# A planned attention kernel: a pace for background steps, either added copy on GpSimd, quartered projections, a new table of limits

## The chip, the cores and the metric

The kernel runs on one core of one Trainium2 chip. The metric is device time in microseconds (us) for one execution. The core has five engines with queues of their own, which wait for each other only by semaphores: TensorE (PE in the profile, with its weight loads as PEld), VectorE (DVE), ScalarE (ACT), GpSimd (POOL), and SyncE (SP), which issues the transfers here. TensorE writes into PSUM, eight banks of 128 x 512 fp32; the other data live in SBUF.

## The reference, cut to what matters

Four layers follow each other, each adding to x (2048 tokens, 512 features, 32 heads of 16 features): A, B, A, B.

```python
x = A_x
x = x + _A_ref(_layernorm(x), A_wq, A_wk, A_wv, A_wo, A_beta)
x = x + _B_ref(_layernorm(x), B_wqkv, B_wo)
x = x + _A_ref(_layernorm(x), A_wq, A_wk, A_wv, A_wo, A_beta)
x = x + _B_ref(_layernorm(x), B_wqkv, B_wo)
```

B is plain attention of all 2048 tokens with all. A cuts the tokens into four segments of 512 with causal attention inside each, and mixes in a memory of the segments before, weighed by a gate g:

```python
logits = jnp.einsum('bhqd,bhkd->bhqk', qs, ks) * scale + mask
a_dot = jnp.einsum('bhqk,bhkd->bhqd', _softmax(logits), vs)
num = jnp.einsum('bhld,bhde->bhle', phi(qs), M)
den = jnp.einsum('bhld,bhd->bhl', phi(qs), z)[..., None] + 1e-06
o = g * (num / den) + (1.0 - g) * a_dot
M = M + jnp.einsum('bhld,bhle->bhde', phi(ks), vs)
z = z + jnp.einsum('bhld->bhd', phi(ks))
```

Both end in a projection with wo. The exponentials of the softmax are most of the work outside TensorE: two B layers have 4 query segments x 4 chunks of heads x 2 x 64 banks of scores each, 4096 in all; two A layers have 16 pairs of groups of 20 banks each, 640 in all.

## The kernel before, in words

The program is one long order of instructions that a planner in Python writes out while it builds. `Sched.estimate` (line 128) keeps an estimated clock for every engine (`sc.t`), and what comes next is decided by comparing these clocks with limits. What the planner estimates never reaches the chip; only the order that it chose does.

*Units.* `attention` (2048) goes through units. A unit takes up to three banks of scores (`take_banks`, 1698): TensorE computes them into one of two sets of three PSUM banks, ScalarE makes the exponential of the unit in one instruction (line 1790), and two units later TensorE multiplies by the values (`pv`, 1810) into a bank of sums. One PSUM bank more (`misc_bank`) serves the projections and everything else in the background.

*VectorE's banks.* Some banks don't go to ScalarE. If `ring_open` (1208) allows, one of a unit's three banks is VectorE's; if `dx_open` (1200) allows, the unit has two banks for ScalarE and two for VectorE, the extra one in `misc_bank`. So 1540 units hold 4736 banks. For such a bank VectorE computes an approximate exponential by integer arithmetic: `dx_first` (1286, recorded at line 1294) reads the scores out of PSUM into a 16-bit number whose bits are a bf16 near the exponential; two added copies, shifted by the constants of `EXP_STEPS` (36 and 84), follow, and TensorE multiplies all three by the values and sums them, in place of one product. The copies are made by `task_dx` (1332) for up to two banks at a time (line 1350) and by `dx_four` (1368) for four (line 1382). The second copy may go to GpSimd: `pool_copy` (1357, recorded at line 1364) treats two 16-bit numbers as one 32-bit integer and adds a constant held in the tile `shift`, provided GpSimd's estimated clock isn't over `POOL_C` ns ahead of VectorE's. It waits for the first copy too (`first`). The three parts are held in the tiles dxt, and, once they are free, in KA, QA, VA and the weights wA and wB.

*Background.* Layer norm, projections, memory, output projections and loads are generators (`task_A` 904, `task_mem` 956, `task_B` 1018, `task_out` 1105, `task_load` 1082) that yield before each step what the step needs, how many column blocks of TensorE and how many ns of VectorE it takes. After each unit `background` (1512) calls `bg_one` (1461), which runs the first step that may go by credits and limits. A projection (`proj_fm` 862, `proj_tm` 874) is four accumulating products of 512 columns, in two pieces: `PART` before a yield of "cont", the rest after it. While a "cont" is open, no four-bank unit starts and the two banks `misc_bank` and `sums_bank` aren't swapped. `wide` is set in `dx_widen` (1263) when the first A layer is done; before it the pieces are always two and two.

*Limits.* `PLAN` (366) has a row for every 20 units ("stretch", `set_limits` 2043); a name that a row doesn't set has its default. Those that the prediction speaks of: POOL_C as above; POOL_XN and POOL_QM give the normalizing step and the query masks to GpSimd; PART and OPART cut projections; PAIRS, NEAR, LOW, R_NEAR say how many banks must be ready ahead before VectorE gets some; DX_LATE, R_LATE, DVE_LATE how far VectorE may lag behind.

The gate for an extra VectorE bank in a unit, as an example of how the limits work:

```python
if not self.RING or self.near < self.rush() and self.pending() or self.low or self.near < self.R_NEAR or self.step - max(self.ring_step, self.dx_step) < self.RGAP or len(self.dx_pairs) - self.dx_waits() > self.R_PAIRS or self.late("act") < self.ACT1:
    return False
```

Of the kernel before, what the change touches and what calls it, by code (L numbers as in the profile page):

```python
# [362 lines left out]
class Builder:  # L363
# [3 lines left out]
        0: dict(TAKEN_A=1, FILL_DVE=200, MASK_PE=800, PE_LOW=7, GAP=3, BG_BANK=400, QMIN=3),  # L367
        1: dict(TAKEN_A=1, FILL_DVE=200, MASK_PE=800, PE_LOW=7, GAP=1, BG_BANK=400, QMIN=3, LOW=20),
        2: dict(EVAC_ACT=800, NEAR=5, SLACK=350, R_NEAR=10, BACK=6, CARRY_W=400, NEARW=40, OPART=3, PAIRS=60, DIV_LATE=2500, BUSY_WAIT=0, TAKEN=0.3, DVE_LATE=800, BUSY_BACK=800, R_PAIRS=2),
        3: dict(EVAC_ACT=800, NEAR=5, SLACK=350, R_NEAR=10, BACK=6, CARRY_W=400, NEARW=40, OPART=3, PAIRS=60, DIV_LATE=2500, BUSY_WAIT=0, TAKEN=0.3, DVE_LATE=800, BUSY_BACK=800, R_PAIRS=2, MARGIN=600),  # L370
        4: dict(MARGIN=500, DX_BANK=900, NEAR=8, SLACK=550, EARLY=300, FILL=0.42, CR_B=1200, PART=3, NEARW=20, PAIRS=60, BUSY_WAIT=0, DX_FIN=3000, POOL_QM=1, POOL_XN=1, EVAC_ACT=800, R_NEAR=10, BACK=6, CARRY_W=400, OPART=3, TAKEN=0.3, DVE_LATE=800, BUSY_BACK=800),
        5: dict(MARGIN=500, DX_BANK=900, NEAR=8, SLACK=550, EARLY=300, FILL=0.42, CR_B=1200, PART=3, NEARW=20, PAIRS=60, BUSY_WAIT=0, DX_FIN=3000, POOL_QM=1, POOL_XN=1, EVAC_ACT=800, R_NEAR=10, BACK=6, CARRY_W=400, OPART=3, TAKEN=0.3, DVE_LATE=800, BUSY_BACK=800, LOW=20),
        6: dict(ACT1=400, NEAR=8, TAKEN_A=1, SLACK=550, PV_SKIP=900, FILL_DVE=200, BACK=8, CR_W=1900, NEARW=20, OPART=2, TAKEN=0.4, LOW=14, DVE_LATE=800, QWAIT=8, HOLD_AT=40, PHI_LATE=0, REST=12),
        7: dict(MARGIN=350, R_LATE=1500, DX_LATE=900, TAKEN_A=1, EARLY=300, CARRY_W=1500, PART=3, OPART=3, MASK_PE=800, GAP=3, QUAD=0, QWAIT=3, HOLD_SEGS=2, POOL_XN=1),
        8: dict(R_LATE=1200, NEARW=40, PAIRS=24, MASK_PE=800, LEVEL=3, TAKEN=0.5, LOW=30, MARGIN=350, TAKEN_A=1, EARLY=300, OPART=3, QUAD=0, FILL=0.47, DX_BANK=900, CR_A=1200),
        9: dict(R_LATE=1200, NEARW=40, PAIRS=24, MASK_PE=800, LEVEL=3, TAKEN=0.5, LOW=30, MARGIN=350, TAKEN_A=1, EARLY=300, OPART=3, FILL=0.47, DX_BANK=900, CR_A=1200, HOLD_SEGS=2),
        10: dict(ACT1=400, DX_BANK=700, NEAR=18, BACK=3, CR_W=1900, CR_B=1800, R_PAIRS=2, PAIRS=24, DIV_LATE=800, DVE_LATE=800),
        11: dict(R_LATE=1500, DX_LATE=900, REST=12, NEAR=8, TAKEN_A=1, R_NEAR=50, PV_SKIP=500, FILL_DVE=400, BUSY_ROOM=900, CR_W=1300, DX_LAG=1, LOW=20, HOLD_SEGS=2, BACK=6),
        12: dict(R_LATE=1500, DX_LATE=900, REST=12, NEAR=8, TAKEN_A=1, R_NEAR=50, PV_SKIP=500, FILL_DVE=400, BUSY_ROOM=900, CR_W=1300, DX_LAG=1, LOW=20, HOLD_SEGS=2, BACK=6, DVE_LATE=800, EARLY=500),
        13: dict(ACT1=600, NEAR=10, PV_SKIP=200, DX_LAG=3, MASK_PE=800, LEVEL=3, DIV_LATE=2500, BG_BANK=100, QUAD=0),  # L380
        14: dict(ACT1=400, REST=16, NEAR=3, SLACK=350, R_NEAR=10, EARLY=0, FILL_DVE=200, BUSY_ROOM=300, CR_B=1800, R_PAIRS=2, PAIRS=999, TAKEN=0.3, QWAIT=8, QMIN=3, HOLD_AT=12, LN1_AT=6, CR_A=1200, MARGIN=500, DVE_LATE=800),
        15: dict(MARGIN=400, NEAR=12, PV_SKIP=100, FILL_DVE=100, BUSY_ROOM=300, FILL=0.55, CR_W=1500, CARRY_W=400, R_PAIRS=2, OPART=3, GAP=3, DVE_LATE=800, QMIN=1, HOLD_AT=40, POOL_QM=1, PAIRS=24),
        16: dict(NEAR=12, BACK=2, CR_W=1300, NEARW=40, DX_LAG=1, DIV_LATE=2500, BUSY_WAIT=0, TAKEN=0.3, DVE_LATE=800, QWAIT=3, QMIN=4, HOLD_MAX=0, PHI_LATE=300, MARGIN=400, FILL_DVE=100, R_PAIRS=2, GAP=3, HOLD_AT=40),
        17: dict(ACT1=200, DX_LATE=500, NEAR=10, PV_SKIP=200, EARLY=500, FILL=0.53, CR_B=1800, CARRY_W=1500, OPART=2, DX_LAG=1, MASK_PE=800, LEVEL=3, DIV_LATE=800, DVE_LATE=800, BG_BANK=100, QUAD=0, LN1_AT=6, POOL_XN=1),
        18: dict(ACT1=400, DX_BANK=700, NEAR=18, BACK=3, CR_W=1900, CR_B=1800, R_PAIRS=2, PAIRS=24, DIV_LATE=800, DVE_LATE=800, EARLY=500, FILL=0.53, CARRY_W=1500, MASK_PE=800, BG_BANK=100, POOL_XN=1),
        19: dict(ACT1=400, DX_BANK=700, NEAR=18, BACK=3, CR_W=1900, CR_B=1800, R_PAIRS=2, PAIRS=24, DIV_LATE=800, DVE_LATE=800, POOL_C=1500),
        20: dict(DX_BANK=900, SLACK=700, PV_SKIP=100, FILL_DVE=200, BUSY_ROOM=300, BACK=10, FILL=0.47, CR_W=1500, PART=3, R_PAIRS=2, TAKEN=0.3, DVE_LATE=800, LN1_AT=3, BUSY_BACK=800),
        21: dict(DX_BANK=900, SLACK=700, PV_SKIP=100, FILL_DVE=200, BUSY_ROOM=300, BACK=10, FILL=0.47, CR_W=1500, PART=3, R_PAIRS=2, TAKEN=0.5, DVE_LATE=800, LN1_AT=3, BUSY_BACK=800, POOL_XN=1),
        22: dict(DX_BANK=900, SLACK=700, PV_SKIP=100, FILL_DVE=200, BUSY_ROOM=300, BACK=6, FILL=0.47, CR_W=1500, PART=3, R_PAIRS=2, TAKEN=0.5, DVE_LATE=800, LN1_AT=3, BUSY_BACK=800, POOL_XN=1, EARLY=300, DIV_LATE=2500),
# [78 lines left out]
    PART = 2  # L468
# [393 lines left out]
    def proj_fm(self, w, bw, off, slot, c, dst, bdst, need=()):  # L862
# [242 lines left out]
    def task_out(self, L, s):  # L1105
        isA = L % 2 == 0
        wo, bwo = (self.woA, self.b_woA) if isA else (self.woB, self.b_woB)
        for ti in range(4):
# [23 lines left out]
            for n, (a, c, ba) in enumerate(srcs):  # L1132
                if half and n == self.OPART:
                    yield ["cont"], NCH - n, 700
# [1065 lines left out]
```

## Time and profile before

| | us |
|---|---|
| median of 3 runs (lowest, highest) | 1719.71 (1719.31, 1720.13) |
| the profiled execution, its own time | 1720.15 |
| its span, first to last instruction | 1718.4 |
| mean granted TensorE clock | 1.00 of full speed |

The page counts an engine as busy while an instruction of it runs; overlapping instructions count once in a group's busy time, and a mean is over single durations, so count times mean can exceed busy. "Idle before, releaser" is the time in which the engine waited just before that group, and what ended it. Stretches of 43 us show where each engine works (columns: TensorE, its weight loads, VectorE, ScalarE, GpSimd, each with its instructions, then the granted clock, the share of the transfer engines and GB/s):

```profile
129.00:172.00 43.00, 40.58 (x534) 16.81 (x528) 34.09 (x72) 43.00 (x37) 10.38 (x13) 1.00 0.10 20
946.00:989.00 43.00, 41.54 (x606) 19.01 (x606) 29.31 (x56) 42.91 (x37) 16.73 (x26) 1.00 0.36 90
1419.00:1462.00 43.00, 39.86 (x411) 10.09 (x407) 41.80 (x64) 42.77 (x48) 25.53 (x26) 1.00 0.03 7
```

VectorE is less busy in the first 300 us, where layer norms and projections must come before there is much attention to do, and again around the middle, where the second pair of layers begins; from about 1250 us on the last layer's attention fills the engines.

### The profile page before, as it was taken

To read this page: it belongs to the slowest core of one execution; us is meant where nothing else is said; L and a number is where in the kernel's file an instruction comes from. 1 tells how busy PE (TensorE), PEld (TensorE's weight loads), DVE (VectorE), ACT (ScalarE), POOL (GpSimd) and SP (SyncE) were. 2 spreads that over 40 slices of the span, in tenths; PEclk is the share of its full clock that TensorE was granted. 3 is DMA by queue.
4 is the path that set the end of the run, shared out by engine and by line. 5 is a ranking of instruction groups with operands and counts; after the bars stand their busy time and mean duration, and the time that the engine had idled before them with its cause. 6 is when DMAs were issued, how large, how long until landed. Compare 5 with 4: busy or idle time off the path is not lost.

```text
span 1718.4 us, 45396 instructions
## 1 busy us (share of the span) xinstructions
PE 1610.9 (94%) x19708; PEld 578.9 (34%) x19775; DVE 1460.6 (85%) x2623; ACT 1681.9 (98%) x1586; POOL 736.1 (43%) x825
## 2 busy tenths in 40 slices
PE   8999899999999999999999999999999999999998
PEld 5543335232222233423342442442222222222236
DVE  6757677989999989789889689797699999998995
ACT  8999999999999999999999999999999999999997
POOL 3222412345557545422413333443266566565651
PEclk9999999999999999999999999999999999999999
DMA  6211202001111000211211311011011100100000
GB/s 179 39 20 20 45 14 33 11 11 26 47 29 26 11 14 20 63 47 26 53 33 45 90 21 50 17 24 35 20 23 23 32 14 7 26 11 11 23 14 18
DMA packets 148425, 54.47 MB, mean 32 GB/s; under 512 B 128768, under 2 KB 147712, under 8 KB 148224
## 3 DMA queue, kind: packets, MB, share of 16 engines
q1 hardware_dynamic: 148224, 51.56, 13.7%
q8 instruction: 155, 2.54, 0.6%
q14 instruction: 46, 0.38, 0.1%
HBM read 18.88 MB, written 2.10 MB: 12 GB/s over the span
## 4 chain that ended last, share of the span: by engine, by line
ACT 67%; PE 17%; DVE 13%; issue 1%; DMA 1%; POOL 1%; SPq 0%; another core or an unknown queue 0%; ACTq 0%; DVEq 0%
ACT pT L1790 65%; PE ps L622 17%; DVE dxt L1294 2%; DVE KA L1294 1%; DVE wA L1294 1%; ACT amem L890 1%; DVE wB L1294 1%; DVE QA L1382 1%; DVE lnst L794 1%; POOL xn L823 0%; SPq L691 0%; DVE wA L1382 0%; DVE dxt L1382 0%; DVE dxt L1350 0%; DMA xT<-xn 0%
## 5 line engine op out<-in xcount | busy, mean ns | idle before, releaser
L1790 ACT ACTIVATE pT<-ps 128x1024 bf16<-128x1024 f32 (+1 forms) x1540 | 1650.2, 1257 | 22.3 <-PE ps L622 19.8
L622 PE MATMUL ps<-qm,KB 32*128 32x512 bf16 x4096 | 565.2, 384 | 72.6 <-ACT pT L1790 47.2
L622 PE MATMUL ps<-pT,VB 128*17 128x512 bf16 x2892 | 494.4, 384 | 1.6 <-DVE dxt L1294 0.5
L622 PEld LDWEIGHTS ps<-qm,KB 32*128 32x128 bf16 x4096 | 144.9, 91 | 595.1 <-ACT pT L1790 476.8
L1294 DVE TENSOR_SCALAR KA<-ps 128x512 uint16<-128x512 f32 (+1 forms) x396 | 291.9, 757 | 14.8 <-PE ps L622 11.8
L1364 POOL TENSOR_TENSOR VA<-KA,shift 128x512 int32<-128x512 int32 (+1 forms) x193 | 200.1, 1047 | 231.0 <-DVE QA L1350 144.6
L1364 POOL TENSOR_TENSOR dxt<-dxt,shift 128x512 int32<-128x512 int32 (+1 forms) x143 | 149.3, 1052 | 282.9 <-DVE dxt L1350 197.5
L1294 DVE TENSOR_SCALAR dxt<-ps 128x512 uint16<-128x512 f32 (+1 forms) x307 | 218.9, 729 | 19.2 <-PE ps L622 17.6
L622 PEld LDWEIGHTS ps<-pT,VB 128*17 128x17 bf16 x2892 | 115.5, 87 | 283.9 <-issue 271.9
L622 PE MATMUL ps<-dxt,VB 128*17 128x512 bf16 x945 | 206.5, 381 | 0.0
L1804 POOL TENSOR_SCALAR_AFFINE_SELECT pT<-pT 128x256 bf16<-128x256 bf16 (+4 forms) x124 | 65.8, 544 | 207.8 <-ACT pT L1790 207.6
L1294 DVE TENSOR_SCALAR wB<-ps 128x512 uint16<-128x512 f32 (+1 forms) x171 | 122.7, 733 | 5.1 <-PE ps L622 4.0
L622 PE MATMUL ps<-QA,VB 128*17 128x512 bf16 x430 | 126.3, 381 | 0.0
L622 PE MATMUL ps<-wB,VB 128*17 128x512 bf16 x534 | 124.2, 381 | 0.0
L1364 POOL TENSOR_TENSOR wA<-wA,shift 128x512 int32<-128x512 int32 (+1 forms) x78 | 81.5, 1057 | 99.5 <-DVE wA L1350 65.2
L622 PE MATMUL ps<-VA,VB 128*17 128x512 bf16 x430 | 119.7, 381 | 1.0 <-POOL VA L1364 1.0
L622 PE MATMUL ps<-KA,VB 128*17 128x512 bf16 x430 | 113.8, 381 | 0.0
L1294 DVE TENSOR_SCALAR wA<-ps 128x512 uint16<-128x512 f32 (+1 forms) x150 | 108.2, 741 | 2.8 <-PE ps L622 2.3
L1364 POOL TENSOR_TENSOR wB<-wB,shift 128x512 int32<-128x512 int32 (+1 forms) x82 | 87.0, 1070 | 51.7 <-DVE wB L1350 33.7
L622 PE MATMUL ps<-qm,KA 32*128 32x128 bf16 (+2 forms) x1536 | 95.1, 254 | 14.0 <-ACT pT L1790 9.8
L622 PE MATMUL ps<-VA,pT 128*128 128x51 bf16 (+1 forms) x2480 | 101.9, 187 | 1.2 <-DVE ob L1887 0.5
L622 PE MATMUL ps<-woB,zero 128*32 128x512 bf16 (+1 forms) x307 | 102.4, 380 | 0.2
(177 smaller groups left out, 2147.9 us busy)
## 6 DMA issues: line engine op xcount, KB each, us to landing
wB<-in_B_wqkv_dram SPq DMA_DIRECT2D x48, 128.0 KB, 2.3
wA<-in_A_wk_dram SPq DMA_DIRECT2D x16, 128.0 KB, 2.3
wA<-in_A_wq_dram SPq DMA_DIRECT2D x16, 128.0 KB, 2.2
wA<-in_A_wv_dram SPq DMA_DIRECT2D x16, 128.0 KB, 2.3
out_dram<-x SPq DMA_DIRECT2D x8, 256.0 KB, 2.3
x<-in_A_x_dram SPq DMA_DIRECT2D x3, 512.0 KB, 8.8
wB<-in_B_wqkv_dram SPq DMA_DIRECT2D x1, 1536.0 KB, 11.9
oT<-ob SPq DMA_TRANSPOSE x63, 2.5
```

The source lines that it names most:

```text
L622: self.sc.add("pe", lambda e: e.matmul(out, lhsT, rhs, start=start, stop=stop, skip_group_check=True), reads=reads, banks=[(bank, "w", all ...
L794: self.op("dve", (lambda i, t: lambda e: e.bn_stats(st[:, k, i, 0:6], self.x[:, t, :]))(i, t), reads=[self.b_x[t]], writes=[bs], ns=690, p ...
L890: self.op("act", lambda e: e.activation(et, src, ACT.Exp), reads=bsrc, writes=self.b_amem, ns=1023, gap=915)
L1294: self.op("dve", lambda e: e.tensor_scalar(d, o, SCALE * LOG2E * 128, 127.0 * 128 + EXP_BIAS, op0=ALU.mult, op1=ALU.add), writes=self.b_dx ...
L1364: self.op("pool", lambda e: e.tensor_tensor(d, s, c, ALU.add), reads=src + [first, self.b_shift], writes=dst, ns=150 + self.POOL_NS * n, g ...
L1382: self.op("dve", (lambda d, s, c: lambda e: e.tensor_scalar(d, s, float(c), None, op0=ALU.add))(d, s, c), reads=self.b_dxs[b] + self.b_dxs ...
L1790: self.sc.add("act", (lambda dst, src: lambda e: e.activation(dst, src, ACT.Exp, scale=SCALE))(dst, src), writes=self.b_pT[slot * 3 + i:sl ...
L1804: self.op("pool", (lambda blk, pat: lambda e: e.affine_select(blk, blk, pattern=pat, compare_op=ALU.is_ge, fill=0.0, base=0, channel_multi ...
```

## The change: what it does

Six things, of which the last is the largest by lines.

1. **Either added copy on GpSimd.** `pool_copy` gets the number k of the copy. For k = 0 it asks POOL_D (0, that is never, unless a row sets it), for k = 1 POOL_C. The tile `shift` holds both constants. A second copy still waits for the first (`[first] * k`).
2. **Pace.** PACE (default 0, off; set in four rows). With it `dx_open` and `ring_open` say no while the last background step with a cost lies more than PACE units back and some step is ready; and `bg_one` no longer holds back steps that cost VectorE nothing when VectorE is late.
3. **Quartered projections.** PART or OPART 0 yields after each of the four products.
4. **Costs** in the planner: a copy on GpSimd 165 + 1.75 n ns (before 150 + 2 n) for n 32-bit numbers; xn on GpSimd 2180 ns (before 800).
5. POOL_NS goes, POOL_D and PACE come.
6. **PLAN**: 77 rows in place of 78. Rows 2, 6, 7, 9, 11, 54 and 67 stay as they were. POOL_D stands in rows 5, 10, 13 to 16, 18, 19, 33, 35 to 37, 39, 40, 48 to 51, 56, 58, 71, 72 and 76; PACE in 0, 4, 42 and 51; PART 0 in 4, 33, 43, 53 and 76; OPART 0 in 0 and 31; a POOL_C over 300 in 27 rows, 0 or 1 in six (before: over 300 in one, 0 or 1 in five).

```diff
@@ PLAN (rows 35, 42, 45 of 77)
-        35: dict(MARGIN=800, NEAR=5, SLACK=350, R_NEAR=10, PART=3, OPART=3, PAIRS=60, DIV_LATE=2500, TAKEN=0.4, DVE_LATE=800, POOL_QM=1),
+        35: dict(MARGIN=500, DX_LATE=700, REST=10, SLACK=350, EARLY=500, FILL_DVE=200, BUSY_ROOM=300, BACK=8, CR_W=1500, R_PAIRS=2, PAIRS=24, DIV_LATE=800, TAKEN=0.3, BG_BANK=100, QWAIT=8, QMIN=4, LN1_AT=6, NEAR=10, HOLD_SEGS=2, ACT1=600, POOL_C=4000, POOL_D=500, OPART=3),
...
+        42: dict(ACT1=200, DX_LATE=500, NEAR=10, PV_SKIP=200, EARLY=500, FILL=0.53, CR_B=1800, CARRY_W=1500, OPART=3, MASK_PE=200, DIV_LATE=800, BG_BANK=100, QUAD=0, LN1_AT=6, FILL_DVE=100, R_LATE=2200, POOL_C=2000, PACE=12),
...
@@ defaults
-    POOL_C, POOL_NS, POOL_WAIT = 300, 2, 100
+    POOL_C, POOL_D, POOL_WAIT = 300, 0, 100
+    PACE = 0
@@ alloc, setup
-        self.shift = sb("shift", [P, 1], dt.int32)
+        self.shift = sb("shift", [P, 2], dt.int32)
-        pool(lambda e: e.memset(self.shift[:, :], EXP_STEPS[1] * 65537), [self.b_shift])
+        for k, c in enumerate(EXP_STEPS):
+            pool((lambda k, c: lambda e: e.memset(self.shift[:, k:k + 1], c * 65537))(k, c), [self.b_shift])
@@ normalize
-                ... **(dict(ns=800, gap=760) if eng == "pool" else dict(ns=448)))
+                ... **(dict(ns=2180, gap=2140) if eng == "pool" else dict(ns=448)))
@@ proj_fm (proj_tm and task_out alike)
-        yield list(need), self.PART if self.wide else 2, 0
+        part = self.PART if self.wide else 2
+        yield list(need), part or 1, 0
...
-            if ci == (self.PART if self.wide else 2):
-                yield ["cont"], NCH - (self.PART if self.wide else 2), 690
+            if ci == part or ci and not part:
+                yield ["cont"], NCH - ci if part else 1, 690 if part or ci == NCH - 1 else 0
@@ new, called at the head of dx_open and ring_open
+    def behind(self):
+        return self.PACE and self.step - self.bg_step > self.PACE and self.pending()
@@ task_dx (dx_four alike)
-                if k and self.pool_copy(d, s, self.b_dxs[b][0:len(ents)], [self.b_dxt[b][k + 1]], self.b_dxt[b][k]):
+                if self.pool_copy(k, d, s, self.b_dxs[b][0:len(ents)], [self.b_dxt[b][k + 1]], self.b_dxt[b][k]):
@@ pool_copy
-        if not now and (not self.POOL_C or self.sc.t["pool"] > self.sc.t["dve"] + self.POOL_C):
+        room = (self.POOL_D, self.POOL_C)[k]
+        if not now and (not room or self.sc.t["pool"] > self.sc.t["dve"] + room):
             return False
...
-        c = bcast(self.shift[:, 0:1], [[0, n]])
-        self.op("pool", ..., reads=src + [first, self.b_shift], writes=dst, ns=150 + self.POOL_NS * n, gap=130 + self.POOL_NS * n)
+        c = bcast(self.shift[:, k:k + 1], [[0, n]])
+        self.op("pool", ..., reads=src + [self.b_shift] + [first] * k, writes=dst, ns=165 + 1.75 * n, gap=145 + 1.75 * n)
@@ bg_one
-        if slack is not None and not pick["next"][1] and self.late("dve") > (...):
+        if slack is not None and not pick["next"][1] and (pick["next"][2] or not self.PACE) and self.late("dve") > (...):
             return False
@@ run
+        if (pe or dve) and task not in self.dx_tasks:
+            self.bg_step = self.step
```

More of the change, by code (lines that the diff above doesn't have):

```diff
@@ L874, in proj_tm @@
     def proj_tm(self, w, bw, off, slot, ti, evac, need=()):
[L875 removed]
+        part = self.PART if self.wide else 2
+        yield list(need), part or 1, 0
         bank, al = self.misc(), self.new_alloc()
@@ L878, in proj_tm @@
         for ci in range(NCH):
-            if ci == (self.PART if self.wide else 2):
-                yield ["cont"], NCH - (self.PART if self.wide else 2), 690
+            if ci == part or ci and not part:
+                yield ["cont"], NCH - ci if part else 1, 690 if part or ci == NCH - 1 else 0
             self.bg_cols += 512
@@ L1124, in task_out @@
                 need.append(self.later())
-            half = self.wide and self.OPART < NCH
-            yield need, self.OPART if half else 4, 0 if half else 700
+            half, part = self.wide and self.OPART < NCH, self.OPART
+            yield need, (part or 1) if half else 4, 0 if half else 700
             t = 4 * s + ti
@@ L1132, in task_out @@
             for n, (a, c, ba) in enumerate(srcs):
-                if half and n == self.OPART:
-                    yield ["cont"], NCH - n, 700
+                if half and (n == part or n and not part):
+                    yield ["cont"], NCH - n if part else 1, 700 if part or n == NCH - 1 else 0
                 self.bg_cols += 512
```

157 lines of the change are left out of this document (78 added, 79 removed).

## The prediction, made before the change was run

> **What bounds the kernel now.** I read the shares of the engines first, then the chain of work that ended last, then the rows of ScalarE.
>
> ```profile
> span 1718.4 us, 45396 instructions
> PE 1610.9 (94%) x19708; PEld 578.9 (34%) x19775; DVE 1460.6 (85%) x2623; ACT 1681.9 (98%) x1586; POOL 736.1 (43%) x825
> ...
> ACT 67%; PE 17%; DVE 13%; issue 1%; DMA 1%; POOL 1%; SPq 0%; another core or an unknown queue 0%; ACTq 0%; DVEq 0%
> ...
> L1790 ACT ACTIVATE pT<-ps 128x1024 bf16<-128x1024 f32 (+1 forms) x1540 | 1650.2, 1257 | 22.3 <-PE ps L622 19.8
> ```
>
> ScalarE (ACT) is busy 98% of the span and nearly all of that is one line, the exponentials of line 1790. It idles 36.5 us in all, 19.8 us of it waiting there for TensorE's scores. So the time falls in two ways only: fewer banks of scores on ScalarE, or fewer of those waits. Two rows split the 1540 units by width:
>
> ```profile
> L1790 ACT ACTIVATE pT<-ps 128x1024 bf16<-128x1024 f32 x1024 | 980.8, 1130 | 5.3 <-PE ps L622 4.1
> L1790 ACT ACTIVATE pT<-ps 128x1536 bf16<-128x1536 f32 x516 | 736.8, 1511 | 17.0 <-PE ps L622 15.8
> ```
>
> That is 1024 x 2 + 516 x 3 = 3596 banks of 512 columns. The work has 4736 (640 of the segmented layers, 4096 of the full ones, from the program), so VectorE (DVE) makes the other 1140. A bank more in a unit costs ScalarE 1511 - 1130 = 381 ns by mean duration, and 736.8/516 - 980.8/1024 = 470 ns by busy time each; I take the middle, 0.425 us. This is the price at which every bank that goes to VectorE is paid back.
>
> What such a bank costs VectorE: its read out of PSUM (line 1294), and two added copies, of which GpSimd (POOL) makes most of the second ones (line 1364).
>
> ```profile
> L1294 DVE TENSOR_SCALAR KA<-ps 128x512 uint16<-128x512 f32 (+1 forms) x396 | 291.9, 757 | 14.8 <-PE ps L622 11.8
> L1364 POOL TENSOR_TENSOR VA<-KA,shift 128x512 int32<-128x512 int32 (+1 forms) x193 | 200.1, 1047 | 231.0 <-DVE QA L1350 144.6
> L1364 POOL TENSOR_TENSOR dxt<-dxt,shift 128x512 int32<-128x512 int32 (+1 forms) x143 | 149.3, 1052 | 282.9 <-DVE dxt L1350 197.5
> L1294 DVE TENSOR_SCALAR dxt<-ps 128x512 uint16<-128x512 f32 (+1 forms) x307 | 218.9, 729 | 19.2 <-PE ps L622 17.6
> ...
> L1294 DVE TENSOR_SCALAR wB<-ps 128x512 uint16<-128x512 f32 (+1 forms) x171 | 122.7, 733 | 5.1 <-PE ps L622 4.0
> ...
> L1364 POOL TENSOR_TENSOR wA<-wA,shift 128x512 int32<-128x512 int32 (+1 forms) x78 | 81.5, 1057 | 99.5 <-DVE wA L1350 65.2
> ...
> L1294 DVE TENSOR_SCALAR wA<-ps 128x512 uint16<-128x512 f32 (+1 forms) x150 | 108.2, 741 | 2.8 <-PE ps L622 2.3
> L1364 POOL TENSOR_TENSOR wB<-wB,shift 128x512 int32<-128x512 int32 (+1 forms) x82 | 87.0, 1070 | 51.7 <-DVE wB L1350 33.7
> ```
>
> The reads take 741.7 us, 0.651 us a bank. GpSimd makes 496 copies of about 1.05 us, two banks each, at most 992 banks; so VectorE makes all 1140 first copies and at least 148 second ones, 1288 in all. The stretches table summed over the span, first line 1350 (pairs), then line 1382 (fours):
>
> ```profile
> 0.00:1718.40 1718.40, 192.71 (x386) 1.00 0.14 32
> ```
>
> ```profile
> 0.00:1718.40 1718.40, 113.35 (x141) 1.00 0.14 32
> ```
>
> 306.1 us / 1288 = 0.238 us for each bank's copy. Where VectorE is short, the stretches show (columns: TensorE, its weight loads, VectorE, ScalarE, GpSimd):
>
> ```profile
> 43.00:86.00 43.00, 39.01 (x630) 23.02 (x641) 30.94 (x89) 38.89 (x33) 11.56 (x22) 1.00 0.24 39
> 215.00:258.00 43.00, 40.21 (x478) 13.78 (x471) 31.89 (x69) 42.75 (x34) 4.45 (x5) 1.00 0.10 14
> 473.00:516.00 43.00, 40.16 (x402) 11.15 (x399) 40.81 (x73) 42.94 (x43) 21.84 (x22) 1.00 0.14 32
> 1075.00:1118.00 43.00, 42.18 (x644) 20.29 (x645) 30.11 (x62) 42.01 (x36) 20.00 (x25) 1.00 0.08 17
> 1376.00:1419.00 43.00, 40.46 (x408) 10.10 (x400) 42.19 (x61) 42.79 (x47) 26.00 (x26) 1.00 0.07 14
> ```
>
> From 473 and from 1376 us VectorE is at 95 to 98% beside a full ScalarE, with GpSimd at 51 to 60%. There VectorE and ScalarE bound the kernel together. At 215 and 1075 us VectorE has a quarter free, and what it may take is set by the limits. At 43 us ScalarE itself lacks 4 us.
>
> **The change, part by part.** *First copies on GpSimd.* POOL_D stands in 23 of 77 rows of the plan, 0.30 of the stretches. With VectorE's banks spread evenly, the first copies there are worth 0.30 x 1140 x 0.238 = 81 us of VectorE. GpSimd takes one only while it is not POOL_D ns ahead of VectorE; both copies of a pair take it about 2.1 us against the 1.3 us of VectorE's two reads, so it falls behind and hands some back. I take half: 40.5 us off VectorE, 85 copies more on GpSimd. Bounds: nothing to all 81 us. *Second copies.* POOL_C is over 300 in 27 rows (1 before). If all left-over second copies there moved, it would be 0.35 x 148 x 0.238 = 12 us; half is 6 us and 13 copies.
>
> *What it costs.* The two engines hinder each other. In order of time near the end:
>
> ```profile
> 1684.39 2.03 POOL L1364 TENSOR_TENSOR VA<-KA,shift 128x512 int32<-128x512 int32 x2 [0.63 <-DVE QA L1382]
> ```
>
> ```profile
> 1685.44 1.28 DVE L1350 TENSOR_SCALAR QA<-KA 128x1024 uint16<-128x1024 uint16 x1
> ```
>
> The copy that begins inside GpSimd's pair ends 0.3 us after it and takes 1.28 us. Usual durations are far shorter (min/median/max in ns):
>
> ```profile
> L1350 DVE TENSOR_SCALAR QA<-KA x123: 293/420/1277, 306.2 to 1688.8; 128x1024 uint16<-128x1024 uint16 x120, 128x512 uint16<-128x512 uint16 x3
> ```
>
> ```profile
> L1382 DVE TENSOR_SCALAR QA<-KA x52: 630/693/1584, 346.7 to 1682.8; 128x2048 uint16<-128x2048 uint16 x52
> ```
>
> At these medians 386 and 141 copies would take 162 + 98 = 260 us; they take 306, so 46 us are lost to such waits, 0.093 us for each of GpSimd's 496 copies. The 98 added ones lose 9 us. Net relief 40.5 + 6 - 9 = 37.5 us. The Trainium skill's page "SBUF — State Buffer" (Who interferes with whom) calls the port pair of the two an exclusive lock, where the second to issue is blocked fully, which the 1.28 us row bears out. By that rule without any planning around it, 98 copies of 1.05 us cover 6% of the span, and 527 VectorE copies would each wait 0.06 x 0.5 us more, 16 us in place of 9, and the sum below would be 2 us worse.
>
> Filled with new banks, relief splits between the engines: a bank takes 0.425 us from ScalarE and adds 0.651 + 0.238 to VectorE, so 37.5 / 1.314 = 28.5 banks, and the time falls by 28.5 x 0.425 = 12 us. Ends: 93 us moved and no waits, -30 us; the other end is the rival below. Each bank also adds two score-times-value matmuls on TensorE, about 57 x 0.2 us; what gives way is filler:
>
> ```profile
> L622 PE MATMUL ps<-woB,zero 128*32 128x512 bf16 (+1 forms) x307 | 102.4, 380 | 0.2
> ```
>
> *Pace.* In four rows (stretches 0, 4, 42, 51) VectorE gets no bank while a ready background step has waited over 2 to 12 units. Rows 0 to 4 lie in the first 150 us, where few banks are VectorE's, so little can be lost; those units go to ScalarE at 0.425 us a bank. What it may bring is earlier projections, and so fewer waits like these, up to 130 us:
>
> ```profile
> ACT pT L1790 <- PE ps L622: 7.6, 17, 1.4
> ```
>
> *Quartered projections.* PART or OPART 0 splits a projection into four pieces, the same matmuls with smaller holes to fit in. The wide phase begins when the freed KA tiles are lent (their first use is at about 304 us), so only the rows from 31 on (31, 33, 43, 53, 76) act. An open projection bars four-bank units and swaps of the sums bank, so it may lose as well; bounds -1 to +2 us by some five banks of 0.425, and I take 0. *Costs in the planner*: xn on GpSimd is now put at 2180 ns,
>
> ```profile
> L823 POOL TENSOR_SCALAR xn<-x,lnst,lnw 128x512 bf16<-128x512 bf16 x13 | 27.4, 2110 | 1.2 <-DMA xT<-xn 0.7 <-DVE lnw L814 0.5
> ```
>
> and a copy at 165 + 1.75 x 512 = 1061 against 1.05 us measured (before 1174): no instruction changes by it, but due times do, the transposes on SP's queue behind xn among them. One more memset of the constants is hidden, since VectorE is waiting for the first input then; uncovered it would cost 0.1 us.
>
> *Limits chosen anew* in 70 rows. No row prices these. Of the 19.8 us of waits for TensorE I take a third away, -6 us. Bounds: all 19.8 gone, or one bank fewer to VectorE in each of 77 stretches, 77 x 0.425 = +33 us.
>
> Sum against the profiled execution's own 1720.15 us (span 1718.4): -12 - 6 = **1702 us**. The median of the runs shown is 1719.71, 0.4 below it, which the rounding covers.
>
> **Rivals.** *The relief isn't used* (1713 us): only where VectorE is at 95% does freed time become banks. If that is half of the stretches and the limits bring 1 us, it is -7. For: the quarter free at 215 and 1075 us. Against: 28.5 banks are few beside 77 stretches. *More banks* (1686 us): the new limits also use VectorE's idle 258 us. One bank more in every second stretch, 38, costs it 34 us and brings 16 us beyond the forecast. For: that idle time. Against: from 1376 us on there is none. *Slower* (1732 us): GpSimd's queue becomes the trap. A copy begun inside its pair is held 0.86 us beyond its median. If each of 98 new copies holds one, 84 us are lost against 46.5 gained, a net 37.5 us on VectorE, 12 us on the whole, and the limits give nothing. GpSimd works in order, so query masks and the output's division stand behind the copies too. It decides from 46.5/98 = 0.47 us a copy, five times today's 0.093. Against: half of GpSimd's time is free. *It doesn't do what it says* (1719 us): GpSimd's gate seldom opens for first copies and the rest balances out.
>
> **How the numbers follow.** Forecast (1694 to 1711) 0.44, unused relief 0.21, more banks 0.13, no effect 0.09, slower 0.13. A difference under 0.2%, 3.4 us, can't be told from none. Faster is 0.44 + 0.21 + 0.13 = 0.78, same 0.09, slower 0.13. The range goes down to the all-copies bound, 1720 - 30 - 6 = 1684, and up to 1722, short of the slower case's full price; about 0.05 lies below and 0.13 above.
>
> **What would show it.** Right: exponentials with some 3560 banks, GpSimd's adds up from 496 to about 600 with many behind a VectorE read of PSUM instead of a VectorE copy, copy medians still 420 and 693 ns with the lost time under 60 us, ScalarE's waits for TensorE near 13 us. Wrong: as many banks on ScalarE as now (the relief went idle), VectorE copies of 1.3 us in number (the trap), or a gain that lies in the first 150 us alone. The forecast falls if GpSimd takes few first copies, or if the time moves more by the limits than by the copies.

## The result, and the profile after

The changed kernel takes 1710.7 us (median of 4 runs, 1708.81 to 1711.88) against 1719.92 us for the one before (4 runs, 1719.31 to 1721.3): a ratio of 0.9944, 95% interval 0.9927 to 0.9961. In a later set of runs it was 1710.36 against 1720.48 us, 0.9942 (0.993 to 0.9955). So it is 9 to 10 us faster; the forecast was 18 faster, and the rival "the relief isn't used" 7. The profiled execution took 1711.88 us, its span 1710.1.

From the page of the changed kernel: span, shares, chain, and the exponentials (now line 1801).

```profile
span 1710.1 us, 45200 instructions
PE 1607.5 (94%) x19545; PEld 573.2 (34%) x19617; DVE 1456.7 (85%) x2618; ACT 1672.4 (98%) x1590; POOL 838.7 (49%) x944
...
ACT 60%; PE 22%; DVE 13%; POOL 2%; DMA 1%; issue 1%; another core or an unknown queue 0%; ACTq 0%; DVEq 0%; POOLq 0%
...
L1801 ACT ACTIVATE pT<-ps 128x1024 bf16<-128x1024 f32 (+1 forms) x1543 | 1640.6, 1234 | 25.4 <-PE ps L622 21.0
```

ScalarE is still the bound at 98%. Its exponentials fell by 1650.2 - 1640.6 = 9.6 us; its waits for TensorE there rose from 19.8 to 21.0. Its whole busy time fell by 1681.9 - 1672.4 = 9.5 us and its whole idle time rose from 36.5 to 37.7 us; together that is the 8.3 us by which the span fell. By width:

```profile
L1801 ACT ACTIVATE pT<-ps 128x1024 bf16<-128x1024 f32 x1065 | 1016.5, 1114 | 8.5 <-PE ps L622 5.8
L1801 ACT ACTIVATE pT<-ps 128x1536 bf16<-128x1536 f32 x478 | 680.6, 1501 | 16.9 <-PE ps L622 15.2
```

1065 x 2 + 478 x 3 = 3564 banks, 32 fewer than before, in 3 units more. VectorE makes 1172. GpSimd's copies (line 1373), with what each waited for:

```profile
L1373 POOL TENSOR_TENSOR VA<-KA,shift 128x512 int32<-128x512 int32 (+1 forms) x188 | 193.9, 1040 | 182.6 <-DVE QA L1358 127.2 <-DVE QA L1391 53.5
L1373 POOL TENSOR_TENSOR dxt<-dxt,shift 128x512 int32<-128x512 int32 (+1 forms) x177 | 186.9, 1064 | 261.2 <-DVE dxt L1358 164.2 <-DVE dxt L1302 56.3 <-DVE dxt L1391 24.3
L1373 POOL TENSOR_TENSOR wA<-wA,shift 128x512 int32<-128x512 int32 (+1 forms) x91 | 98.5, 1088 | 53.6 <-DVE wA L1391 19.0 <-DVE wA L1358 18.3 <-DVE wA L1302 15.3
L1373 POOL TENSOR_TENSOR wB<-wB,shift 128x512 int32<-128x512 int32 x78 | 84.2, 1091 | 34.0 <-DVE wB L1358 16.9 <-DVE wB L1391 13.0 <-DVE wB L1302 4.0
L1373 POOL TENSOR_TENSOR QA<-KA,shift 128x512 int32<-128x512 int32 (+1 forms) x69 | 77.5, 1129 | 66.5 <-DVE KA L1302 66.4
```

603 copies against 496. The new sort is seen by its releaser: a first copy waits for VectorE's read of PSUM (line 1302) where a second one waits for a VectorE copy (1358, 1391); the group QA is new as a whole. By the program 160 are first copies and 443 second ones. VectorE's own copies, the sums over the span for line 1358 (pairs) and line 1391 (fours):

```profile
0.00:1710.10 1710.10, 189.77 (x373) 1.00 0.15 32
```

```profile
0.00:1710.10 1710.10, 84.58 (x110) 1.00 0.15 32
```

274.4 us, 31.7 less than before. The medians have not moved (min/median/max of one tile's copies in ns):

```profile
L1358 DVE TENSOR_SCALAR QA<-KA x112: 278/420/1257, 322.4 to 1694.5; 128x1024 uint16<-128x1024 uint16 x107, 128x512 uint16<-128x512 uint16 x5
L1391 DVE TENSOR_SCALAR QA<-KA x34: 675/693/1542, 451.0 to 1648.3; 128x2048 uint16<-128x2048 uint16 x34
```

**Where in time.** The banks that ScalarE and VectorE had begun by a given time, each counted once by the start of its instruction, show it. The kernel before is 43 banks ahead of the changed one at 860 us, 26 at 1118 us and 17 at 1204 us, but 10 behind at 1290 us, and 15 at 1634 us. So the new order first falls behind and then overtakes. At 1710 / 4736 = 0.36 us a bank, the 27 banks between 1204 and 1290 us are 10 us, as much as the whole gain; 18 of them come in the first 21.5 us. The stretches of these 21.5 us show why, first before and then after (columns: TensorE, weight loads, VectorE, ScalarE, GpSimd):

```profile
1204.00:1225.50 21.50, 20.35 (x246) 6.18 (x242) 7.59 (x12) 19.98 (x16) 1.18 (x3) 1.00 0.08 26
```

```profile
1204.00:1225.50 21.50, 20.86 (x242) 5.66 (x238) 18.05 (x29) 21.50 (x22) 16.52 (x18) 1.00 0.04 8
```

At the passage to the last layer the old order puts projections in a row on TensorE; few scores are ready, so VectorE gets no bank and stands at 35%. In the new order it is at 84% there.

### The profile page after: what moved, and what is told of

It reads as the page before. It is cut to its first block, busy times and chain, and to the rows that moved or that the text cites. A ratio compares the mean times of both kernels' runs of the same rounds, so it can differ in the third digit from the quotient of the medians.

```text
span 1710.1 us, 45200 instructions
## 1 busy us (share of the span) xinstructions
PE 1607.5 (94%) x19545; PEld 573.2 (34%) x19617; DVE 1456.7 (85%) x2618; ACT 1672.4 (98%) x1590; POOL 838.7 (49%) x944
## 4 chain that ended last, share of the span: by engine, by line
ACT 60%; PE 22%; DVE 13%; POOL 2%; DMA 1%; issue 1%; another core or an unknown queue 0%; ACTq 0%; DVEq 0%; POOLq 0%
ACT pT L1801 58%; PE ps L622 22%; DVE KA L1302 2%; DVE wA L1302 1%; DVE wB L1302 1%; DVE dxt L1302 1%; ACT amem L893 1%; DVE lnst L795 1%; DVE dxt L1358 0%; DVE xn L824 0%; DMA xT<-xn 0%; POOL dxt L1373 0%; DMA phq<-amem 0%; POOL wB L1373 0%; DVE QA L1358 0%
## 5 line engine op out<-in xcount | busy, mean ns | idle before, releaser
L1801 ACT ACTIVATE pT<-ps 128x1024 bf16<-128x1024 f32 (+1 forms) x1543 | 1640.6, 1234 | 25.4 <-PE ps L622 21.0
L1302 DVE TENSOR_SCALAR KA<-ps 128x512 uint16<-128x512 f32 (+1 forms) x448 | 319.1, 731 | 18.0 <-PE ps L622 15.3
L1373 POOL TENSOR_TENSOR dxt<-dxt,shift 128x512 int32<-128x512 int32 (+1 forms) x177 | 186.9, 1064 | 261.2 <-DVE dxt L1358 164.2
L1302 DVE TENSOR_SCALAR dxt<-ps 128x512 uint16<-128x512 f32 (+1 forms) x321 | 227.6, 725 | 19.6 <-PE ps L622 17.2
L1815 POOL TENSOR_SCALAR_AFFINE_SELECT pT<-pT 128x256 bf16<-128x256 bf16 (+4 forms) x146 | 74.0, 521 | 215.2 <-ACT pT L1801 215.0
L622 PE MATMUL ps<-QA,VB 128*17 128x512 bf16 x465 | 138.7, 382 | 0.4 <-POOL QA L1373 0.3
L1373 POOL TENSOR_TENSOR wA<-wA,shift 128x512 int32<-128x512 int32 (+1 forms) x91 | 98.5, 1088 | 53.6 <-DVE wA L1391 19.0
L1302 DVE TENSOR_SCALAR wB<-ps 128x512 uint16<-128x512 f32 (+1 forms) x143 | 109.0, 782 | 5.4 <-PE ps L622 4.2
L1373 POOL TENSOR_TENSOR QA<-KA,shift 128x512 int32<-128x512 int32 (+1 forms) x69 | 77.5, 1129 | 66.5 <-DVE KA L1302 66.4
L622 PE MATMUL ps<-wB,VB 128*17 128x512 bf16 x498 | 104.5, 381 | 0.3 <-POOL wB L1373 0.2
```

The costliest lines, as they stand in the source:

```text
L622: self.sc.add("pe", lambda e: e.matmul(out, lhsT, rhs, start=start, stop=stop, skip_group_check=True), reads=reads, banks=[(bank, "w", all ...
L1302: self.op("dve", lambda e: e.tensor_scalar(d, o, SCALE * LOG2E * 128, 127.0 * 128 + EXP_BIAS, op0=ALU.mult, op1=ALU.add), writes=self.b_dx ...
L1373: self.op("pool", lambda e: e.tensor_tensor(d, s, c, ALU.add), reads=src + [self.b_shift] + [first] * k, writes=dst, ns=165 + 1.75 * n, ga ...
L1801: self.sc.add("act", (lambda dst, src: lambda e: e.activation(dst, src, ACT.Exp, scale=SCALE))(dst, src), writes=self.b_pT[slot * 3 + i:sl ...
L1815: self.op("pool", (lambda blk, pat: lambda e: e.affine_select(blk, blk, pattern=pat, compare_op=ALU.is_ge, fill=0.0, base=0, channel_multi ...
```

## The experiments

"Planned anew" means that the program was built with an edit, so that all later decisions could change; "in the same order" means that the changed kernel's instructions were written out again one by one, in its order, with only the named ones altered. Times are medians, ratios are to the kernel before.

| run | us | ratio (95%) | banks on ScalarE | its waits for TensorE, us |
|---|---|---|---|---|
| before | 1720 to 1721 | 1 | 3596 | 19.8 |
| changed kernel, again (e5) | 1710.36 | 0.9942 (0.9930 to 0.9955) | 3564 | 20.4 |
| first copies back, same order (e1) | 1725.66 | 1.0033 (1.0019 to 1.0046) | 3564 | 31.0 |
| one near-tie (e2) | 1718.43 | 0.9988 (0.9979 to 0.9998) | 3571 | 22.5 |
| another near-tie (e10) | 1714.63 | 0.9966 (0.9952 to 0.9979) | 3574 | 20.5 |
| rows 48 to 58 of before (e4) | 1719.26 | 0.9990 (0.9980 to 0.9999) | 3576 | 23.3 |
| without quarters (e11) | 1731.73 | 1.0063 (1.0047 to 1.0078) | 3592 | 31.5 |
| without pace (e8) | 1733.66 | 1.0078 (1.0064 to 1.0092) | 3578 | 35.2 |
| without first copies (e7) | 1755.89 | 1.0204 (1.0189 to 1.0220) | 3610 | 36.3 |
| whole old table (e3) | 1761.11 | 1.0238 (1.0223 to 1.0253) | 3640 | 37.8 |

### What the copies are worth

**e1, first copies back on VectorE, same order.** All banks stay where they are.

```diff
+        back = (lambda d, s, v: lambda e: e.tensor_scalar(d, s, float(v), None, op0=ALU.add))(d, s, EXP_STEPS[k])
...
+        if not k:
+            self.alt[id(o)] = back
...
+        replay(self, lambda op, eng, fn, reads: ("dve", self.alt[id(op)], [x for x in reads if x is not self.b_shift]) if id(op) in self.alt else (eng, fn, reads))
```

> Same order and same banks as the changed kernel; only the 160 first copies that GpSimd makes are put back on VectorE, in place. That is about 160 x 0.42 = 67 us more for VectorE and 168 us less for GpSimd. Theory 'copies pay' (the relief is what lets VectorE hold its banks): VectorE is 95% busy in about half of the span, and the order can't give banks back to ScalarE, so 25 to 40 us longer, 1735 to 1750. Theory 'relief unused' (the copies were moved where VectorE had time): less than 10 us longer, under 1720, with VectorE's idle time smaller by the whole 67 us.

It took 1725.66 us (1724.54 to 1728.74), 15 us more than the changed kernel, between the two expectations. The sums over the span of the same 373 pair copies, the 160 returned ones and the 110 fours:

```profile
0.00:1725.40 1725.40, 180.71 (x373) 1.00 0.15 32
```

```profile
0.00:1725.40 1725.40, 69.38 (x160) 1.00 0.15 32
```

```profile
0.00:1725.40 1725.40, 82.53 (x110) 1.00 0.15 32
```

The returned copies cost VectorE 69.4 us, and the others became 274.4 - 263.2 = 11.1 us shorter with 160 fewer copies on GpSimd: a copy there costs VectorE's copies 11.1 / 160 = 0.069 us. The medians say the same: 274.4 - 373 x 0.420 - 110 x 0.693 = 41.5 us lost, over 603 copies 0.069. VectorE's whole busy time rose by only 1492.9 - 1456.7 = 36.2 us, while the durations of all its instructions, added up one by one, rose by 55 us; the difference is ends of neighbouring instructions that overlap, which the whole counts once and the groups twice. ScalarE has the same banks, so it pays in waits:

```profile
L1831 ACT ACTIVATE pT<-ps 128x1024 bf16<-128x1024 f32 (+1 forms) x1543 | 1644.7, 1225 | 36.5 <-PE ps L648 31.0
```

Idle there rose from 25.4 to 36.5 us, and the busy time of the line by 4.1 us; together that is the 15 us. A dip of the granted clock at 1309 to 1315 us (below) has a part in the profiled execution. "The relief isn't used" is out for this order. But 15 us is what the copies are worth in an order made for them.

**e7, no first copies, planned anew.**

```diff
-        ... POOL_D=2500 ...
+        ...
```

> POOL_D taken out of all rows, so that GpSimd makes no first copy and everything is planned anew. If the first copies carry the gain, it is at least as slow as the fixed order with these copies back on VectorE (1725.7 us): 1722 to 1765 us, the upper end if the table's limits stand on these copies being cheap, as the old table under the new costs gave 1761 us. If what matters is only that some order was chosen, it is like the near-tie run: 1716 to 1722 us.

(The diff stands for all 23 rows.) 1755.89 us (1754.34 to 1756.79), 45 us over the changed kernel, with 3610 banks on ScalarE. That is 30 us worse than the same copies put back by hand, so most of it isn't the copies: without them the planner takes other turns, and the table doesn't suit these. The clearest is seen in ScalarE's timeline:

```profile
1385.93 6.95 ACT L1801 ACTIVATE pT<-ps 128x1536 bf16<-128x1536 f32 x7 [6.24 <-PE ps L622]
```

The changed kernel has no such idle stretch of over 2 us between 800 and 1600 us, nor has the one before.

### Does the table suit one order?

**e2, a near-tie.** The limit that admits a second copy to GpSimd, 1 ns off where no row sets it.

```diff
-    POOL_C, POOL_D, POOL_WAIT = 300, 0, 100
+    POOL_C, POOL_D, POOL_WAIT = 301, 0, 100
```

> Control: the default of POOL_C is 301 in place of 300, nothing else; the planner takes a near-tie the other way once and its order differs from there on. Theory 'copies pay': the kinds and numbers of instructions stay within a few, so 1711 within 3 us. Theory 'one chosen order' (the table is fitted to the one order that it was chosen on): over 5 us longer, 1716 or more, as far as the change itself moved the time.

1718.43 us (1716.43 to 1721.52): 8 us of the 9 to 10 are gone.

**e10, another near-tie.**

```diff
-    FILL_DVE = 300
+    FILL_DVE = 305
```

> Another near-tie: one default of the program, FILL_DVE, 305 instead of 300, so that the order is planned anew with the same costs, table and copies. If the changed table suits one exact order, this loses as the first near-tie did (1718.4 us): 1712 to 1722 us. If that one was a mishap: 1709 to 1712 us.

1714.63 us (1714.4 to 1716.16): 4 us gone, with 3574 banks on ScalarE and the same waits; 10 banks at 0.425 us are the 4 us.

**e3, the old table under the changed program.** Rows without POOL_D, PACE or quarters, but the new planning costs of a copy and of xn.

> The changed code with the table of before: no POOL_D, no PACE, no PART or OPART of 0, so of the change only the planner's two costs (xn 2180, copies 1061) act. Theory 'copies pay': without first copies on GpSimd nothing is gained and nothing lost, 1720 within 4 us. Theory 'one chosen order': the old table no longer fits an order planned with other costs, 1740 or more, though the work is the same.

1761.11 us (1760.35 to 1763.27), 40 us slower than the kernel before, from the same table. What differs are the planning costs. So the old table doesn't suit the new costs; whether a near-tie alone would move the old order as far wasn't tried.

**e4, rows 48 to 58 as before** (units 960 to 1179, some 1130 to 1350 us, the stretch where the gain lies).

> The changed kernel with the rows 48 to 58 of before; the order is the same up to unit 960, about 1050 us. Theory 'one chosen order': the gain lies in the passage to the last layer at 1160 to 1290 us, where VectorE is 39 of 43 us busy after and 31 before; it goes again, 1718 to 1724, with a stretch there in which VectorE is under 70% busy. Theory 'copies pay': only the first copies of those rows are lost, some 50, 50 x 0.42 x 0.32 = 7 us at most if half of the rows' relief was used 3 to 4 us, so 1713 to 1716 and no such stretch.

1719.26 us (1716.77 to 1721.43), the gain gone, but not where I expected. This order is 16 banks ahead of the changed kernel at 1290 us, with VectorE at 90% or more in every 21.5 us since 1161; it is 12 behind at 1376 us and 19 at 1634. It loses its lead in one place: 17 banks ahead at 1333 us, it is 6 behind at 1354, and there VectorE is at 69%. A dip of the granted clock at 1348.0 to 1351.4 us lies in that place in its profile.

### Pace and quarters

**e8, without pace.** PACE taken out of all four rows; taken out of rows 0, 4 and 51 alone it leaves the same instructions in the same order, so only row 42 acts.

> PACE taken out of all rows (only row 42's bears on the order of the instructions). If the pace is worth something by itself, VectorE reads fewer banks after row 42 and ScalarE's waits for TensorE grow: over 1722 us. If it acts as one near-tie does, the loss is like that of the near-tie run, some 7 us: 1714 to 1722 us. If it does nothing: 1709 to 1713 us.

**e11, without quarters in row 33.** In rows 0, 4, 31, 43, 53 and 76 the quarters change no instruction's place.

```diff
-        33: dict(MARGIN=600, NEAR=12, SLACK=350, R_NEAR=10, PART=0, ...
+        33: dict(MARGIN=600, NEAR=12, SLACK=350, R_NEAR=10, ...
```

> PART=0 taken out of row 33, the only one in which it changes the instructions' order (its projection is then made in halves as the defaults have it). My forecast gave the quartered projections nothing. If that holds and the table suits one exact order, the loss is like that of a near-tie, 1712 to 1722 us; if the quarters carry a gain of their own, over 1724 us.

e8 took 1733.66 us (1731.69 to 1735.94) and e11 1731.73 us (1729.69 to 1733.78), 23 and 21 us over the changed kernel: more than the near-ties cost, and by the words put down beforehand a worth of their own. Where they lose speaks against that. Banks ahead of the changed kernel's profile at the same time, counted as above:

```
us      before    e2    e4    e8   e11
 860      +43    +11   +11   +11     0
1118      +26     +9    +9    +3    +1
1204      +17     +9   +19    -4   -19
1290      -10    +10   +16   -12   -26
1333       -6     +9   +17   -12   -25
1376      -10     +4   -12   -40   -48
1634      -15    -13   -19   -61   -60
```

Row 33 is reached at some 780 us and row 42 at some 990 (units 660 and 840 of the 1543, by the exponentials done). Up to 860 us e2, e4 and e8 still have the changed kernel's order; 6 of their 11 banks arise by 80 us, where its profile has two clock dips (below). e11 is level until 1118 us and loses 27 banks by 1290; e8 loses 23 between 860 and 1290. Both, and e4 as well, then lose 23 to 29 banks (8 to 10 us) in the same 43 us from 1333 us, for e8 and e11 hundreds of us behind their rows. What stands there, in e8, on ScalarE, then on TensorE:

```profile
1360.43 4.20 ACT L1801 ACTIVATE pT<-ps 128x1536 bf16<-128x1536 f32 x4 [5.93 <-PE ps L622]
```

```profile
1353.29 1.25 PE L622 MATMUL ps<-woB,oT 128*32 128x512 bf16 x16
1355.33 1.05 PE L622 MATMUL ps<-woB,oT 128*32 128x512 bf16 x16 [0.80 <-DVE x L1140]
1357.17 1.05 PE L622 MATMUL ps<-woB,oT 128*32 128x512 bf16 x16 [0.79 <-DVE x L1140]
1359.01 1.05 PE L622 MATMUL ps<-woB,oT 128*32 128x512 bf16 x16 [0.79 <-DVE x L1140]
1359.99 0.61 PE L622 MATMUL ps<-qm,KB 32*128 32x512 bf16 x6
```

Four output projections of 16 matmuls stand in a row, each behind VectorE's eviction of the last one from the one PSUM bank, and the next scores (qm,KB) come behind all four. The changed kernel makes the same four earlier and apart, with scores between; VectorE's evictions there:

```profile
1309.61 0.69 DVE L1140 TENSOR_TENSOR x<-x,ps 128x512 bf16<-128x512 bf16 x1 [0.36 <-PE ps L622]
1316.09 0.69 DVE L1140 TENSOR_TENSOR x<-x,ps 128x512 bf16<-128x512 bf16 x1
1321.85 0.68 DVE L1140 TENSOR_TENSOR x<-x,ps 128x512 bf16<-128x512 bf16 x1
1330.56 0.68 DVE L1140 TENSOR_TENSOR x<-x,ps 128x512 bf16<-128x512 bf16 x1
```

The 6.24 us of e7 have the same evictions of line 1140 in the chain of waits; so have the 2.64 us of e11 and the 2.23 us of e4 before their next exponentials at 1361 and 1346 us.

**e12, e8's order with scores between the four.** The score matmuls of the next units are put between the projections; the rest of e8's order is kept.

```diff
+    for u, to in zip(units, starts[1:]):
+        for k in u:
+            e = log[k]
+            j = k
+            while j > to + b.hoisted and not clash(log[j - 1], e):
+                j -= 1
...
+            log.insert(j, log.pop(k))
+            if j == to + b.hoisted:
+                b.hoisted += 1
```

> The instructions of e8_no_pace (1733.7 us) in its order but for one place: at 1353 to 1360 us its profile has four output projections in a row on TensorE, 16 matmuls each, with VectorE's eviction of one between it and the next, while ScalarE waits 5.93 us for a bank. Here the score matmuls of the two ScalarE units that came behind all four, and three of the third's, stand between them. If that row of projections is what the removed pace cost there, ScalarE's idle time between 1333 and 1376 us falls from 8.0 us to under 3, and the time to 1726 to 1730 us. If the row only showed that banks were missing for another reason (the copies and the query masks queued on GpSimd just before it), the wait moves behind it and the time stays within 1731 to 1736 us.

1736.78 us (1734.54 to 1737.71), 3 us over e8 and above both ranges put down. One unit went ahead; then the wait was back:

```profile
1359.44 1.45 ACT L1868 ACTIVATE pT<-ps 128x1536 bf16<-128x1536 f32 x1 [0.41 <-PE ps L688]
1367.37 1.94 ACT L1868 ACTIVATE pT<-ps 128x1024 bf16<-128x1024 f32 x2 [6.48 <-PE ps L688]
```

The second unit's scores were made at 1360.85 us. Its exponentials go into tiles pT whose old values TensorE still had to multiply, and these products I had left behind the projections:

```profile
1360.85 0.39 PE L688 MATMUL ps<-qm,KB 32*128 32x512 bf16 x3
...
1366.21 0.60 PE L688 MATMUL ps<-qm,KB 32*128 32x512 bf16 x1 [1.60 <-DVE ub L1994]
1366.74 1.02 PE L688 MATMUL ps<-pT,VB 128*17 128x512 bf16 x5
```

ScalarE starts at 1367.37 us, just behind the first of them. Of the wait, 1.60 us is TensorE's own for VectorE (ub, line 1994). So the experiment doesn't decide: late scores alone aren't the wait, but whether the row of projections with its late products is, wasn't tried.

### The granted clock

The runs of the changed kernel spread over 3 us, and its first profile shows the granted clock low in two places. Each is shown with the 3.41 us before it (last columns: clock, share of the transfers, GB/s):

```profile
40.99:44.40 3.41, 2.01 (x41) 1.36 (x40) 2.51 (x7) 3.41 (x4) 0.00 (x0) 1.00 0.00 0
44.40:47.81 3.41, 3.19 (x48) 2.31 (x49) 0.81 (x3) 2.71 (x3) 1.57 (x4) 0.50 0.02 5
64.88:68.29 3.41, 1.78 (x18) 0.71 (x15) 3.20 (x12) 1.82 (x2) 0.94 (x2) 1.00 0.00 0
68.29:71.70 3.41, 3.41 (x38) 1.83 (x39) 1.02 (x2) 1.45 (x2) 0.00 (x0) 0.50 0.38 77
```

**e5, the changed kernel again.**

> The changed kernel unaltered, beside the runs below on one chip. 1708 to 1713 us; if the spread of its times comes from dips of the granted clock, the runs whose mean clock is 1.000 lie near 1709 us and each hundredth of clock lost (of 1710 us) shows as 1 to 2 us per 0.001.

1710.36 us (1709.06 to 1711.68); this profile had a dip at 67.6 to 71.0 us and none at 44. Over both sets of runs those with a mean clock of 1.000 took 1708.81 and 1709.06 us, the others (0.997 to 0.999) 1709.7 to 1711.88.

**e6, more zeros in TensorE's gaps, same order.**

```diff
+        n = min(512, int(room * MORE * 2.4) // 64 * 64)
+        if room > 100 and n >= 64:
...
+            sc.log.insert(len(sc.log) - 1, ("pe", new.fn, [], [], [], new.name, [], 0, None, None, new))
```

> The instructions of the changed kernel in the same order on the same engines, with 153 matmuls of zeros more on TensorE (about 16 us of it) where the program expects it idle for over 0.1 us. If the dips of the granted clock follow TensorE's short idles, they come more seldom: median 1708 to 1710 us, mean clock 1.000 in nearly every execution. Rival: the zeros stand ahead of score matmuls that are already late, so that ScalarE waits longer: 1712 to 1720 us. Rival: neither, 1710 to 1712 us.

1710.95 us (1710.3 to 1714.46), the same as e5 within the spread, and its profile has both dips (0.50, at 45.3 and 69.2 us). The second rival, neither, holds.

**e9, zeros in the gaps at 38 to 76 us, same order.**

```diff
+                if idle > 250 and 36000 < op.end < 76000 and banks:
+                    for _ in range(int(idle / 215)):
...
+                        new.add("pe", (lambda z: lambda e: e.matmul(z, b.zero[:, 0:128], b.woB[:, 0, :], start=False, stop=False, skip_group_check=True))(z),
```

> The instructions of the changed kernel in the same order, with 16 matmuls of zeros more between 38 and 76 us, each 128x512, in TensorE's idle stretches of over 0.25 us while it waits for ScalarE or VectorE (42 and 66 to 68 us among them, where the profiles of this kernel show its granted clock fall to 0.50 to 0.60). If the idle stretches bring the dips, none is left before 76 us, and the median comes to that of the executions at clock 1.000: 1708 to 1709.5 us. Rival: the dips come however long TensorE idles, by its busy stretches: they stay, 1710 to 1712 us.

1715.47 us (1713.35 to 1716.51), ratio 0.9966 (0.9953 to 0.9978), so 5 us slower than the changed kernel. The zeros go into the bank of the matmul that waits, and so wait for the same thing: the gap ahead of them stayed (1.30 us at 43.2 us), and they came on top; a dip at 69.1 us was left. It isn't the test that it was meant to be. What the traces do show of the dips stands in the last section.

## Why the prediction was right, and where not

**The time** was inside the range (1684 to 1722) and on the right side, but 9 us from the forecast and nearer to the rival with 1713 us. The range is 38 us wide and holds the times of three rivals too, so that lying inside it says little for the mechanism. Of the two terms of the sum, -12 and -6, the first came as -9.6 and the second not at all.

**Copies moved: the sum right, its parts not.** I forecast 85 first copies and 13 second ones more on GpSimd, 98; it was 107, but as 160 first and 53 second ones fewer. By `pool_copy` a first copy that GpSimd takes moves its estimated clock ahead, so that the next second copy is more likely to stay with VectorE. VectorE's copies fell by 31.7 us with the new banks' copies in them; the forecast is 37.5 less 28.5 x 0.238 = 6.8 us for its new banks, 30.7.

**Their price to VectorE** was mis-sized in the safe direction: 0.069 us a copy on GpSimd, shown in two ways, against the forecast's 0.093 us. Lost time went from 46 us, with GpSimd busy 43% of the span, to 41.5 us at 49%. What is lost is lost by copies that begin inside one of GpSimd's: by the traces 115 of VectorE's 527 before, at 0.44 us each over the median, and 131 of 483 after, at 0.33 us. So more are held, but for less. The longest copy in the row above, 1257 ns, is one: it begins 0.06 us into a GpSimd copy at 704.03 us. That fits the exclusive lock of the Trainium skill ("SBUF — State Buffer", Who interferes with whom). The prediction's estimate from that lock, 16 us for 98 copies begun regardless of GpSimd, is 0.16 us each, over twice what e1 shows.

**The banks** came as forecast: 32 instead of 28.5 to VectorE, 3564 on ScalarE against "some 3560". Their price was right too, though no row that I took it from measures it. Where exponentials follow each other, one begins before the last has ended, so durations overlap. Rows without idle time show what each adds, first two banks a unit, then three, in the kernel before:

```profile
1383.72 23.93 ACT L1790 ACTIVATE pT<-ps 128x1024 bf16<-128x1024 f32 x26
```

```profile
1202.92 16.22 ACT L1790 ACTIVATE pT<-ps 128x1536 bf16<-128x1536 f32 x12
```

These are 0.92 and 1.35 us each. Over the whole trace the end of an exponential lies 917 ns behind the last one's with two banks and 1343 ns with three (medians, the same before and after), so a bank costs 426 ns; that the middle of 381 and 470 met it was luck. The 32 banks are then 13.6 us, and only 9.6 came, because more exponentials begin after an idle time: 121 instead of 96, and such a one adds about 0.11 us more. That is about 3 of the missing 4 us. e1, with the same units and 163 such starts, has 4.1 us more on the same line.

**The limits** were the failed step. "Of the 19.8 us of waits for TensorE I take a third away" stood on no row, and none went: 21.0 us. What the new table does, the runs show: under the new planning costs the old one gives 1761 us, and one limit changed by 1 ns gives 1718. It is fitted to one exact order. My own test, "the forecast falls if the time moves more by the limits than by the copies", thus has two answers: within one order the copies move it by 15 us and the banks stay; over the whole, the table, with the copies that it allows, moves it by 50. The copies are the part with a mechanism. That the net gain is 9 to 10 and not 15 I read as the balance of two fitted orders; no run shows it by itself.

**Pace and quarters** I put at nothing, with small bounds for the quarters (-1 to +2 us), of which I held that the rows from 31 on act. Of the rows with PART or OPART 0 only 33 acts, of those with PACE only 42. Taken out, each costs over 20 us, ten times that bound, but most of the loss comes over 300 us behind the row, at other work. As a price of the thing itself the zero is neither shown nor refuted; as a bound on an edit to such a planner it was far too narrow.

**The rivals.** "More banks" and "slower" are out: GpSimd's copies didn't become a trap, VectorE lost less to each than before. "It doesn't do what it says" is out by the 160 first copies.

## What to carry to other kernels

Where a program plans its order by comparing clocks with tuned limits, first ask what a change of no meaning does (here 4 and 8 us), and price an edit by writing the same order out again with only that edit; planning anew measures the table. In such an order look for the longest single waits of the bounding engine: four of the slower orders here (e4, e7, e8, e11) have one of 2 to 6 us where output projections stand in a row on one PSUM bank, and the changed kernel has none there. It isn't the only way to be slow: e2 has no such wait either, and the slowest, e3, has a wait of 3.75 us at 974 us and none at that place. A price per unit of work is to be taken from how far the ends of neighbouring instructions lie apart, not from their durations.

## What the runs showed of the hardware

Between 20 us and the end of the work, every dip of the granted clock in these profiles is to 0.50 of full speed and 3.41 us long; in e1 two follow each other, from 1308.7 to 1315.5 us. They differ between executions of the same instructions: the changed kernel had dips at 44.4 and 68.3 us in one profile and at 67.6 us alone in another. Executions of the changed kernel with a mean clock under 1.000 took 1 to 3 us more than those at 1.000.

Where a profile has several dips, their starts lie whole multiples of 3.413 us apart: 7 between 44.40 and 68.29 us, 229 between 66.44 and 848.09 us in e11, 380 between 68.85 and 1365.91 us in e12. So in these profiles the clock changes on a grid of fixed steps, and where the grid lies differs by execution. In the step before each of the 19 dips TensorE was busy 0.22 to 0.75 of the time, as in the rows under "The granted clock" (2.01 and 1.78 of 3.41 us), against 0.94 over the span. A sparse step isn't enough: in e7 the step up to 1385.0 us on that profile's own grid was at 0.53, and the clock stayed at 1.00. Which sparse steps bring a dip is open.

Nor is a short idle stretch of TensorE enough. The kernel before has the same gap with a full clock behind it, the changed one a dip; the rows are the first matmuls behind the gap, before and after, and then the clock of the kernel before:

```profile
43.37 0.39 PE L622 MATMUL ps<-qm,KA 32*128 32x512 bf16 x3 [0.98 <-ACT pT L1790]
```

```profile
42.63 0.40 PE L622 MATMUL ps<-qm,KA 32*128 32x128 bf16 x12 [0.99 <-ACT pT L1801]
```

```profile
43.00:46.00 3.00, 2.58 (x57) 1.86 (x59) 1.17 (x3) 3.00 (x4) 0.00 (x0) 1.00 0.02 5
46.00:49.00 3.00, 2.93 (x57) 1.89 (x55) 2.78 (x7) 3.00 (x3) 0.61 (x1) 1.00 0.10 21
```

And in one order a GpSimd copy of 128x512 32-bit numbers costs VectorE's copies the same 0.07 us each, whether 443 or 603 are made; in the order of the kernel before it is 0.093 us with 496.
